# A gated-linear-attention and maxout kernel: w_out loaded whole ahead of w1, two sums of w2·w_out placed in the scores' banks, a first token group of two chunks, and another build-time order

## The chip, the cores and the metric

The kernel runs on one core of one Trainium2 chip. The metric is the device time of an execution in microseconds. The kernel before takes 147.35 us, the median of four runs (146.59, 146.69, 148.02 and 148.11). The profile is of one execution, which took 146.59 us.

The engines are called as in the profile: PE is TensorE (PEld its weight loads), DVE is VectorE, ACT is ScalarE, POOL is GpSimd, and SP is SyncE, whose queue (SPq) issues nearly all the transfers.

## The reference

Two steps follow each other. The first is a linear attention with a decaying state, for 4 batches of 8 heads, 768 positions and a head size of 48:

```python
for t in range(S):
    state = alpha[:, :, t, :, None] * state + np.einsum('bhd,bhe->bhde', k[:, :, t], v[:, :, t])
    y[:, :, t] = np.einsum('bhd,bhde->bhe', q[:, :, t], state)
```

Its output, with heads and head size joined, is x: 3072 tokens of 384 numbers. The second step is a feed-forward block with the larger of two projections, w1 and w2 of 384 x 1024 and w_out of 1024 x 384:

```python
g = np.maximum(x @ w1, x @ w2)
out = (g @ w_out).astype(np.float32)
```

Inputs and output are float32.

## The kernel before, in words

**The mathematics.** The larger of two numbers is written as max(a, b) = relu(a - b) + b. So the kernel computes h = x(w1 - w2), takes g = relu(h), and the output is g·w_out + x·M with M = w2·w_out. wd is w1 - w2 in float16, made on VectorE (`prep_wd`, L667, one instruction for each half of the 1024 columns). M is a matrix of 384 x 384 that is made once: w2 is cast (`prep_w2`), transposed by TensorE (`prep_t`, L677, the tile wtp) and copied to w2T (`prep_te`); w_out is cast (tile wo); then `prep_m` (L691, tile mp) sums eight matmuls for each of three blocks of rows, four in a first half (i = 0) and four in a second (i = 1), and the result is copied to m (operation `mev`).

**The attention in chunks.** Positions go in chunks of 128, 24 in all. In a chunk, the logarithms of alpha are summed by a matmul (cs), and exponentials of the sums with both signs (ep, en) scale q and k (qt and kt). These are transposed (tp), copied out (qk), and multiplied to scores (pa and pb, in two banks); the scores are masked on VectorE (pt), and y is summed from pt·v and from q times the state carried in (T, made by POOL from w and a decay). y is copied by ScalarE to xT. The first six chunks go in three double chunks, called d0, d1 and d2, by their own functions and with a d ahead of the tile's name: dloga, dcs, den, dep, dqt, dkt, dtp, dqk, dpa and dpb, dpt, dkv, dw, dT, dy.

**The feed-forward in groups.** Up to three finished chunks make a group. `fstep` (L702) makes h for 128 of the 1024 columns with three matmuls, so a group has eight such blocks of h; `relu` (L707 on VectorE, L709 on ScalarE) makes g. `tstep` makes the output of one chunk in a bank: three matmuls of x·M (L716) and eight of g·w_out (L719). The last chunk goes in two halves of columns (`tcols`). The output is evicted (L663, tile outs) and stored.

**Banks.** Three pools share the eight accumulation banks: psx with three (cs, tp, kv, wtp), psp with two (the scores pa and pb) and psm with three (y, h, op, and mp).

**Transfers.** All loads go through SP's queue in an order fixed by a chain of `after`: d0 in seven pieces, then w2 in two halves, w_out's first half, w1 in two halves, w_out's second half, d1, d2, and then the single chunks, four transfers each. The single chunks reuse the memory that held the weights in float32.

**Who sets the order.** No order is written by hand. Each piece of work is an `Op` with the engines that may run it, an assumed cost on each, what it depends on, the buffers that it takes, and a priority. `Sched.run` plays the program at build time: it keeps an assumed clock for each engine, picks the operation that can start first (a lower `prio` wins among equals), adds its cost, and emits its instructions. The order of instructions on each engine, and the choice between ScalarE and VectorE, thus follow from assumed costs; on the chip each engine runs its list strictly in that order. For a load, the assumed landing is made from the cost on a wire that all loads share (`LOAD`, `WLOAD / 2`, `DL`) and a latency (`lat`). For h and output work there is `refill`: it looks which chunks' xT is finished, and forms the next group of up to three. Chunk work has priorities near the chunk's number, h and output work 1000 and above, the sums of M 0.4.

Of the kernel before, what the change touches and what calls it, by code (L numbers as in the profile page):

```python
# [1 line left out]

# [7 lines left out]
FP32 = mybir.dt.float32  # L11
# [4 lines left out]
class Op:  # L16


    def __init__(self, sched, name, n, engs, fn, deps=(), lat=0.1, alloc=(), reads=(), prio=0.0, tiled=False, after=(), slack=0.0):
        self.name, self.n, self.engs, self.fn, self.lat = name, n, engs, fn, lat  # L20
        self.deps, self.alloc, self.prio, self.tiled = [d for d in deps if d is not None], list(alloc), prio, tiled
        self.after = [d for d in after if d is not None]
        self.done, self.slack = None, slack
        for b in list(alloc) + list(reads):
            b.users.append(self)
        for e in engs:
            sched.todo[e].append(self)
# [19 lines left out]
        return max(u.done for u in old.users)  # L47


class Sched:  # L50


# [4 lines left out]
    def __init__(self):  # L57
        self.todo = {e: [] for e in ("PE", "ACT", "DVE", "POOL", "SP")}
        self.free = {e: 0.0 for e in self.todo}
        self.wire = 0.0  # L60
        self.tiled = False
        self.refill = None

    def start(self, op):
        t = 0.0
# [42 lines left out]
    def run(self):  # L108
        while True:
            c = self.pick("PE")  # L110
            if c and self.refill:
                self.refill(c[1], c[1] > self.free["PE"] + 0.3)
            best = None
            for e in self.todo:
                c = self.pick(e)
                if c and (best is None or c[1] < best[0]):
                    best = (c[1], e, c[2])
            if best is None:
                if self.refill and self.refill(1e9, True):
                    continue  # L120
                break
            t, e, op = best
            cost = op.engs[e]
            if e == "PE" and t < 19.0:
                cost *= 1.9
            if e == "PE" and op.tiled != self.tiled:
                cost += 0.09
                self.tiled = op.tiled
            if e == "SP":
                t = max(t, self.wire - 4.0)  # L130
                self.wire = max(self.wire, t + 0.7) + cost
                op.done = self.wire + op.lat
                cost = 0.45
            else:
                op.done = t + cost + op.lat
            self.free[e] = t + cost
            for b in op.alloc:
                b.ring.taken.append(b)
            for x in op.engs:
                self.todo[x].remove(op)  # L140
            op.fn(e)
        assert not any(self.todo.values()), {e: [(o.name, o.n) for o in v][:5] for e, v in self.todo.items()}
# [3 lines left out]
def kernel(  # L146
# [23 lines left out]
    C = 128  # L170
# [5 lines left out]
    NT, DM = out.shape  # L176
    DFF = moe_w1.shape[1]
    NF = DFF // 128
    WMAX = 384
# [7 lines left out]
    psp = ctx.enter_context(tc.tile_pool(name="psp", bufs=2, space=bass.MemoryType.PSUM))  # L187
    psm = ctx.enter_context(tc.tile_pool(name="psm", bufs=3, space=bass.MemoryType.PSUM))
# [495 lines left out]
    mps = [None] * 3  # L684

    def prep_m(s, i):
        if i == 0:
            mps[s] = psm.tile([128, DM], FP32, tag="m", name="mp")
        mp = mps[s]
        for f in range(NFH * i, NFH * i + NFH):  # L690
            nc.tensor.matmul(mp, lhsT=w2T[:, f, s * 128 : (s + 1) * 128], rhs=wo16[:, f, :],  # L691
                             start=(f == 0), stop=(f == NF - 1))
# [62 lines left out]
    rx, rp, rm = Ring(3), Ring(2), Ring(3)  # L755
# [6 lines left out]
    def op(*a, **k):  # L762
        return Op(S, *a, **k)
# [3 lines left out]
    def dep(n, name):  # L767
        return G[n].get(name) if n in G else None

    LOAD, WLOAD = 1.06, 3.9  # L770
    bl = {}

    def loads_of(n):
# [9 lines left out]
    prev = None  # L783

    def dloads_of(m, margin):
# [3 lines left out]
        for i, h in parts:  # L789
            prev = op("dld", m, {"SP": DL / (1 if h is None else 2)}, lambda e, i=i, h=h: dload(m, i, h), lat=1.6 + margin,  # L790
                      alloc=[dbl[m][i]] if not h else (), reads=[dbl[m][i]] if h else (), after=[prev], prio=0.3 + m)
            for x in (0, 1):
                if h is None or h == x:
                    GD[m]["ld", i, x] = prev

    lw2, lw1, lwo = [None] * 2, [None] * 2, [None] * 2
    for x in "d0 w20 w21 wo0 w10 w11 wo1 d1 d2".split():
        if x[0] == "d":
            dloads_of(int(x[1]), 0.3 * int(x[1]))
        else:  # L800
            i = int(x[2])
            fn, to = {"w2": (load_w2, lw2), "wo": (load_wo, lwo), "w1": (load_w1, lw1)}[x[:2]]
            prev = to[i] = op(x, i, {"SP": WLOAD / 2}, lambda e, i=i, fn=fn: fn(i), lat=1.6, after=[prev], prio=0.5)


    w2c = [[op("w2c", (s, i), c, lambda e, s=s, i=i: prep_w2(e, s, i), deps=[lw2[i]], prio=-0.5)
# [13 lines left out]
    w2t = []  # L820
    for f in range(0, NF, 2):
        b = Buf(rx)
        t = op("w2t", f, {"PE": 0.4}, lambda e, f=f: prep_t(f), lat=0.17, deps=w2c[f // NFH], alloc=[b], prio=f - 10)
        w2t.append(op("w2te", f, {"DVE": 0.6, "ACT": 0.75}, lambda e, f=f: prep_te(e, f), deps=[t], reads=[b], prio=-0.4))
    mdone, mfirst = [], []
    for s in range(3):
        b = Buf(rm)
        prev = None
        for i in range(2):
            prev = op("m", s, {"PE": 0.66}, lambda e, s=s, i=i: prep_m(s, i), lat=0.17,  # L830
                      deps=w2t[2 * i : 2 * i + 2] + woc[2 * i : 2 * i + 2], after=[prev] if i else [],
                      alloc=[b] if i == 0 else (), reads=[b] if i else (), prio=0.4 + 0.01 * s)
            if i == 0:
                mfirst.append(prev)
        mdone.append(op("mev", s, {"ACT": 0.4, "DVE": 0.45}, lambda e, s=s: copy(e, m16[:, s, :], mps[s]),
                        deps=[prev], reads=[b]))
# [11 lines left out]
    for m in range(ND):  # L848
# [67 lines left out]
            alloc=[("y", 0), ("y", 1)], reads=[("pt", 0), ("pt", 1), ("qk", 0), ("qk", 1), "v", "T"], tiled=True)  # L916
        if m == 0:
            for o in mfirst:
                o.after.append(g["p4", 0])
        for u in range(2):  # L920
            G[2 * m + u]["a3"] = add("a3", u, {"ACT": 0.5}, lambda e, m=m, u=u: dx(m, u), [g["p4", 0]], reads=[("y", u)])

# [55 lines left out]
    def refill(now, idle):  # L978
        while pend and pend[0].done is not None:
            pend.pop(0)  # L980
        if len([o for o in pend if o.done is None]) > 2 or nxt[0] >= NCG:
            return
        if wdc[0][0].done is None or wdc[0][0].done > now + 0.3:
            return
        a = nxt[0]
        k = 0
        while k < WMAX // C and a + k < NCG and G[a + k]["a3"].done is not None and G[a + k]["a3"].done <= now + 0.3:
            k += 1
        if k == 0 or (k < WMAX // C and not idle):
            return  # L990
        nxt[0] += k
        W, a0 = k * C, a * C
        bg = Buf(rg16)
        rel = []
        xs = [G[a + i]["a3"] for i in range(k)]
        for f in range(NF):
            bh = Buf(rm)
            o = op("f", a, {"PE": 3 * max(W / 2400 + 0.0025, 0.07)}, lambda e, a0=a0, W=W, f=f: fstep(a0, W, f),
                   lat=0.17, deps=xs + wdc[f // NFH], after=pend[-1:], alloc=[bh] + ([bg] if f == 0 else []), prio=1000 + a)
            pend.append(o)  # L1000
            rel.append(op("relu", a, {"ACT": 0.08 + W / 1200, "DVE": 0.1 + W / 960},
                          lambda e, a0=a0, W=W, f=f: relu(e, a0, W, f), deps=[o], reads=[bh, bg], prio=n))
        for i in range(k):
            bo, bs = Buf(rm), Buf(ro)
            if a + i == NCG - 1:

                for c in range(2):
                    b = (bo, Buf(rm))[c]
                    o = op("t", a + i, {"PE": 0.95}, lambda e, a0=a0, i=i, c=c: tcols(a0, i, c), lat=0.17,
                           deps=mdone + woc + rel, after=pend[-1:], alloc=[b], reads=[bg], prio=1000 + a)  # L1010
                    pend.append(o)
                    ev = op("oev", a + i, {"ACT": 0.28}, lambda e, t=a0 + i * C, c=c: ocols(e, t, c), deps=[o],
                            alloc=[] if c else [bs], reads=[b, bs] if c else [b], prio=n)
                    op("st", a + i, {"ACT" if c else "SP": 0.3}, lambda e, t=a0 + i * C, c=c: scols(t, c), lat=1.2, deps=[ev],
                       reads=[bs], prio=-1)
                continue
            for half in range(2):
                o = op("t", a + i, {"PE": (0.98, 0.82)[half]}, lambda e, a0=a0, i=i, half=half: tstep(a0, i, half),
                       lat=0.17, deps=mdone + woc + (rel[:3] if half == 0 else rel), after=pend[-1:],
                       alloc=[bo] if half == 0 else (), reads=[bg] if half else [bg], prio=1000 + a)  # L1020
                pend.append(o)
            ev = op("oev", a + i, {"ACT": 0.4, "DVE": 0.45}, lambda e, t=a0 + i * C: oevict(e, t), deps=[o],
                    alloc=[bs], reads=[bo], prio=n)
            op("st", a + i, {"SP": 0.55}, lambda e, t=a0 + i * C: store(t), lat=1.2, deps=[ev], reads=[bs], prio=-1, slack=3.0 if a + i < NCG - 4 else 0.0)
        return True
# [34 lines left out]
```

## Time and profile before

| what | value |
|---|---|
| median of four runs | 147.35 us |
| the profiled execution: its own time / its span | 146.59 us / 144.8 us |
| busy PE / ACT / DVE / POOL | 130.7 / 99.0 / 86.5 / 83.5 us |
| PE idle in 0:10, 10:20, 20:30, 30:40 us of the span | 6.7, 2.5, 1.9, 0.0 us |
| h, op with w_out, op with M: matmuls and busy time | 216, 36.7 us; 184, 35.4 us; 69, 15.0 us |
| sums of M (mp): matmuls, first and last start | 24, 19.2 and 25.5 us |
| DMA: bytes, mean rate | 28.62 MB, 198 GB/s |

The span is the time from the first to the last instruction; the run's own time is longer by what lies around it. A busy time counts the time in which at least one instruction was under way; matmuls overlap, and a row's mean duration is that of one matmul from issue to modelled end, so the distance from start to start is the better measure of their cost. Forty slices of 3.62 us each show an engine's busy share in tenths. In a list of instructions, brackets give the idle time of the engine ahead of one, and what released it.

### The profile page before, as it was taken

What the parts mean: (1) busy time and instruction counts of PE and PEld (TensorE: products, weight loads), DVE (VectorE), ACT (ScalarE), POOL (GpSimd) and SP (SyncE); (2) the same over time, 40 slices, a digit from 0 to 9 for tenths busy, and PEclk for the clock granted to TensorE, in tenths of its full rate; (3) what the DMA queues carried; (4) which work ended last, traced back from release to release, by engine and by line L of the source; (5) the groups of instructions that cost most, each with busy time, mean ns of one, the idle gap of its engine ahead of it and who ended that gap; (6) DMA issues with size and microseconds to landing.
All of it is one profiled execution on the core that took longest, in us unless ns stands there. A gap on an engine that the chain in (4) does not pass through costs nothing.

```text
span 144.8 us, 4890 instructions
## 1 busy us (share of the span) xinstructions
PE 130.7 (90%) x1969; PEld 89.7 (62%) x1969; DVE 86.5 (60%) x163; ACT 99.0 (68%) x222; POOL 83.5 (58%) x184
## 2 busy tenths in 40 slices
PE   0375796899999999999999999999999999999991
PEld 0354653677777787666666667676666676556671
DVE  4648783688496679578539766699638854300000
ACT  4444844787686897879777977685768676825831
POOL 7997400587999788675559865657576955000000
PEclk9999999999999999999999999999999999999999
DMA  4999999999989797999999999999999722010213
GB/s 117 266 347 386 386 341 228 267 266 198 182 173 262 156 198 177 217 201 190 233 239 182 251 239 190 209 210 260 183 207 238 189 76 103 6 54 9 104 54 109
DMA packets 93686, 28.62 MB, mean 198 GB/s; under 512 B 87904, under 2 KB 92128, under 8 KB 93664
## 3 DMA queue, kind: packets, MB, share of 16 engines
q1 hardware_dynamic: 93520, 28.22, 81.9%
q8 instruction: 15, 0.25, 0.7%
q10 hardware_dynamic: 144, 0.10, 0.2%
q14 instruction: 7, 0.06, 0.1%
HBM read 23.59 MB, written 4.72 MB: 196 GB/s over the span
## 4 chain that ended last, share of the span: by engine, by line
PE 80%; DMA 9%; SPq 6%; ACT 2%; DVE 1%; issue 1%
PE h L702 22%; PE op L719 21%; DMA wof<-in_moe_w_out_dram 9%; PE op L716 8%; PE y L473 6%; PE pa L414 4%; PE tp L396 3%; SPq L231 3%; PE tp L398 3%; SPq L211 2%; PE cs L338 2%; PE kv L425 2%; PE dy L635 2%; PE mp L691 1%; PE dtp L541 1%; PE cs L342 1%
## 5 line engine op out<-in xcount | busy, mean ns | idle before, releaser
L702 PE MATMUL h<-xT,wd 128*128 128x384 f16 (+1 forms) x216 | 36.7, 308 | 0.0
L719 PE MATMUL op<-wo,g 128*128 128x384 f16 x184 | 35.4, 326 | 0.0
L709 ACT ACTIVATE g<-h 128x384 f16<-128x384 f32 (+1 forms) x53 | 24.1, 472 | 3.1 <-PE h L702 2.4
L702 PEld LDWEIGHTS <-wd 128*128 128x128 f16 x216 | 19.5, 97 | 9.3 <-issue 0.4
L719 PEld LDWEIGHTS <-g 128*128 128x128 f16 x184 | 17.2, 98 | 11.4
L663 ACT COPY outs<-op 128x384 f32<-128x384 f32 x20 | 9.6, 481 | 15.9 <-PE op L719 15.9
L433 DVE TENSOR_TENSOR pt<-pa,u 128x512 f16<-128x512 f32 x18 | 12.4, 690 | 7.7 <-PE pb L414 6.3
L375 POOL TENSOR_TENSOR T<-w,g 48x192 f16<-48x192 f32 x30 | 15.4, 514 | 1.1
L663 ACT COPY qk<-tp 128x1024 f16<-128x1024 f16 x14 | 14.2, 1016 | 2.3 <-PE tp L398 2.2
L716 PE MATMUL op<-m,xT 128*128 128x384 f16 x69 | 15.0, 326 | 0.0
L529 POOL TENSOR_TENSOR dkt<-dkf,den 128x384 f16<-128x384 f32 x6 | 6.3, 1050 | 10.9 <-ACT den L511 10.9
L433 DVE TENSOR_TENSOR pt<-pb,u 128x512 f16<-128x512 f32 x18 | 12.2, 680 | 0.1
L444 DVE TENSOR_TENSOR w<-kv,t 48x192 f32<-48x192 f32 x24 | 8.5, 352 | 5.9 <-PE kv L425 4.6
L707 DVE TENSOR_SCALAR g<-h 128x256 f16<-128x256 f32 (+1 forms) x19 | 9.0, 483 | 3.9 <-PE h L702 3.7
L348 ACT ACTIVATE en<-cs 128x384 f32<-128x384 f32 x18 | 8.9, 496 | 2.2 <-PE cs L342 2.2
L360 POOL TENSOR_TENSOR kt<-w2f,en 128x384 f16<-128x384 f32 x6 | 6.0, 1001 | 7.2 <-issue 2.6
L360 POOL TENSOR_TENSOR kt<-wof,en 128x384 f16<-128x384 f32 x6 | 6.5, 1087 | 6.1 <-ACT en L348 4.5
L477 ACT CAST xT<-y 128x384 f16<-128x384 f32 x18 | 8.7, 482 | 1.9 <-PE y L473 1.4
L360 POOL TENSOR_TENSOR kt<-w1f,en 128x384 f16<-128x384 f32 x6 | 6.0, 1002 | 5.5 <-issue 3.7
L473 PE MATMUL y<-pt,v 128*32 128x128 f16 x288 | 9.0, 220 | 0.0
L348 ACT ACTIVATE ep<-cs 128x384 f32<-128x384 f32 x18 | 8.9, 495 | 0.0
L716 PEld LDWEIGHTS <-xT 128*128 128x128 f16 x69 | 6.1, 98 | 3.1
(127 smaller groups left out, 281.5 us busy)
## 6 DMA issues: line engine op xcount, KB each, us to landing
out_dram<-outs SPq DMA_DIRECT2D x23, 192.0 KB, 3.3
w2f<-in_moe_w_dram SPq DMA_DIRECT2D x2, 768.0 KB, 7.2
wof<-in_moe_w_out_dram SPq DMA_DIRECT2D x2, 768.0 KB, 11.2
w1f<-in_moe_w_dram SPq DMA_DIRECT2D x2, 768.0 KB, 11.2
dvf<-in_v_dram SPq DMA_DIRECT2D x3, 384.0 KB, 5.9
wof<-in_alpha_dram SPq DMA_DIRECT2D x6, 192.0 KB, 3.8
wof<-in_k_dram SPq DMA_DIRECT2D x6, 192.0 KB, 4.1
wof<-in_q_dram SPq DMA_DIRECT2D x6, 192.0 KB, 4.5
```

The source lines that it names most:

```text
L348: nc.scalar.activation(out=t, in_=csv, func=ACTF.Exp, scale=scale)
L360: nc.gpsimd.tensor_mul(out=kts[n % NB][:, :, 0:D], in0=loads[n][1], in1=st[n]["en"])
L375: nc.gpsimd.tensor_mul(out=st[n]["T16"][ps, :, D * t : D * t + D], in0=st[n - 1]["w"][ps], in1=st[n]["g"][ps].unsqueeze(2).to_broadcast([D ...
L433: nc.vector.tensor_mul(out=s["pt"][:, t], in0=s["pp"][t], in1=ub)
L473: nc.tensor.matmul(y[o : o + 32, b // 4, :], lhsT=lhsT, rhs=rhs, start=start, stop=stop)
L477: nc.scalar.copy(out=xT[:, :, n * C : (n + 1) * C], in_=st[n]["y"])
L663: {"ACT": nc.scalar.copy, "DVE": nc.vector.tensor_copy, "POOL": nc.gpsimd.tensor_copy}[e](out=out, in_=in_)
L702: nc.tensor.matmul(h[:, 0:W], lhsT=wd16[:, s, f * 128 : (f + 1) * 128], rhs=xT[:, s, a : a + W], start=(s == 0), stop=(s == 2))
L707: nc.vector.tensor_relu(gts[a][:, f, 0:W], hs[a, f][:, 0:W])
L709: nc.scalar.activation(out=gts[a][:, f, 0:W], in_=hs[a, f][:, 0:W], func=ACTF.Relu)
L716: nc.tensor.matmul(op, lhsT=xT[:, s, t0 : t0 + C], rhs=m16[:, s, :], start=(s == 0), stop=False)
L719: nc.tensor.matmul(op, lhsT=gts[a][:, f, i * C : (i + 1) * C], rhs=wo16[:, f, :], start=False, stop=(f == NF - 1))
```

## The change

Five things change in the code.

- **Order of the loads.** The second half of w_out moves ahead of both halves of w1. The assumed cost of a weight load goes from 3.9 to 4.1 (for two halves) and its assumed latency from 1.6 to 2.0, 2.8 for w1's second half; the latency added for d0, d1 and d2 goes from 0, 0.3 and 0.6 to 0.2, 0.5 and 1.2.
- **Banks of mp.** The first two of the three mp tiles are taken from psp, the pool of the scores, and the third from psm as before.
- **Order of the sums of M.** Before, all first halves come after dy of d0 (`p4`) by the `after` list. Now they come after the second scores of d0 (`p3`, 1), and only the third tile's also after dy. The first halves of the first two tiles keep their priority; the third tile's first half and all second halves get 900. The third tile now depends on all of w2T and of wo.
- **First group.** `refill` may form the first group when two chunks are ready even where PE is not idle in the plan.
- **Jitter.** Each operation's assumed cost is multiplied by a factor drawn between 0.85 and 1.15 from a generator with a fixed seed. Only the planned times change by it.

```diff
@@ class Op
-        self.done, self.slack = None, slack
+        self.done, self.slack, self.scale = None, slack, 1.0 + JITTER * (sched.rng.random() - 0.5)
...
+SEED, JITTER = 107, 0.3
...
+        self.rng = random.Random(SEED)
@@ Sched.run
-            cost = op.engs[e]
+            cost = op.engs[e] * op.scale
@@ prep_m
-            mps[s] = psm.tile([128, DM], FP32, tag="m", name="mp")
+            mps[s] = (psp, psp, psm)[s].tile([128, DM], FP32, tag="ppm"[s], name="mp")
@@ loads
-    LOAD, WLOAD = 1.06, 3.9
+    LOAD, WLOAD = 1.06, 4.1
...
+    LANDS = {"w11": 2.8}
...
-    for x in "d0 w20 w21 wo0 w10 w11 wo1 d1 d2".split():
+    for x in "d0 w20 w21 wo0 wo1 w10 w11 d1 d2".split():
...
-            dloads_of(int(x[1]), 0.3 * int(x[1]))
+            dloads_of(int(x[1]), (0.2, 0.5, 1.2)[int(x[1])])
...
-            prev = to[i] = op(x, i, {"SP": WLOAD / 2}, lambda e, i=i, fn=fn: fn(i), lat=1.6, after=[prev], prio=0.5)
+            prev = to[i] = op(x, i, {"SP": WLOAD / 2}, lambda e, i=i, fn=fn: fn(i), lat=LANDS.get(x, 2.0), after=[prev], prio=0.5)
@@ sums of M
+    MPRIO = 900
     for s in range(3):
-        b = Buf(rm)
+        b = Buf((rp, rp, rm)[s])
...
-                      deps=w2t[2 * i : 2 * i + 2] + woc[2 * i : 2 * i + 2], after=[prev] if i else [],
-                      alloc=[b] if i == 0 else (), reads=[b] if i else (), prio=0.4 + 0.01 * s)
+                      deps=(w2t + woc if s == 2 else w2t[2 * i : 2 * i + 2] + woc[2 * i : 2 * i + 2]), after=[prev] if i else [],
+                      alloc=[b] if i == 0 else (), reads=[b] if i else (), prio=(0.4 if i == 0 and s < 2 else MPRIO) + 0.01 * s)
@@ double chunks
             for o in mfirst:
-                o.after.append(g["p4", 0])
+                o.after.append(g["p3", 1])
+            mfirst[2].after.append(g["p4", 0])
@@ refill
-        if k == 0 or (k < WMAX // C and not idle):
+        if k == 0 or (k < WMAX // C and not idle and (a or k < 2)):
```

More of the change, by code (lines that the diff above doesn't have):

```diff
@@ L2 @@
+import random
 from contextlib import ExitStack
```

## The prediction

> **What bounds the kernel now.** I read the page first: busy time per engine, then the forty slices.
>
> ```profile
> span 144.8 us, 4890 instructions
> PE 130.7 (90%) x1969; PEld 89.7 (62%) x1969; DVE 86.5 (60%) x163; ACT 99.0 (68%) x222; POOL 83.5 (58%) x184
> PE   0375796899999999999999999999999999999991
> DMA  4999999999989797999999999999999722010213
> ```
>
> TensorE (PE) is short of its span by 14.1 us, and the slices put nearly all of that into the first eight (3.62 us each). The busy times by stage say it in numbers (PE's busy time is the second figure after the stage):
>
> ```profile
> 10.00:20.00 10.00, 7.48 (x161) 5.68 (x158) 8.07 (x13) 5.84 (x11) 5.01 (x10) 1.00 1.05 383
> 20.00:30.00 10.00, 8.10 (x69) 5.51 (x68) 6.06 (x9) 5.93 (x15) 3.10 (x4) 1.00 1.07 260
> 30.00:40.00 10.00, 10.00 (x239) 7.20 (x240) 6.84 (x14) 7.16 (x20) 8.43 (x17) 1.00 1.06 210
> ```
>
> Idle PE: 6.7 us in 0:10, 2.5 in 10:20, 1.9 in 20:30, then none until the last matmul, and 3.0 us for the last eviction and store. So from 30 us on the end is a sum of PE work; only idle time ahead of it can go, unless the order inside the dense stretch hides small stalls. What the idle pieces are is in PE's list of instructions in order of time (start, length, then in brackets the idle time and its releaser):
>
> ```profile
> 12.94 0.80 PE L677 MATMUL wtp<-ident,w 128*128 128x128 f16 x6 [0.76 <-DVE dw L599]
> 15.22 0.31 PE L558 MATMUL dpa<-dqk 48*64 48x128 f16 x2 [1.48 <-ACT dqk L663]
> ...
> 19.25 3.26 PE L691 MATMUL mp<-wo,w2T 128*128 128x384 f16 x12
> 23.72 2.11 PE L691 MATMUL mp<-wo,w2T 128*128 128x384 f16 x12 [1.21 <-ACT wo L663]
> ...
> 26.53 1.14 PE L702 MATMUL h<-xT,wd 128*128 128x256 f16 x9
> 28.37 0.40 PE L541 MATMUL dtp<-ident,dqt 128*128 128x128 f16 x4 [0.69 <-DVE dqt L527]
> ```
>
> The 1.9 us of 20:30 are two waits: 1.21 for the second half of wo, 0.69 for dqt. The first is a transfer at bottom; the ScalarE list shows it, and a second case of the same kind:
>
> ```profile
> 13.63 0.62 ACT L663 CAST w<-w2f 128x512 f16<-128x512 f32 x1 [1.42 <-DMA w2f<-in_moe_w_dram]
> 14.16 1.01 ACT L663 COPY dqk<-dtp 128x1024 f16<-128x1024 f16 x1
> 22.84 0.83 ACT L663 CAST wo<-wof 128x768 f16<-128x768 f32 x1 [2.38 <-DMA wof<-in_moe_w_out_dram]
> ```
>
> dqk's input was whole at 12.18 (end of its transposes), but the copy stood behind a cast that waited for w2's second half.
>
> **The loads.** Issue plus time to landing of each: w2 first half 11.5, second 13.6, wo first 15.7, w1 17.8 and 19.8, wo second 22.8; then d1 (alpha 24.15, k 25.5, q 26.8, v 28.5). DMA is full from 2 us on, so a permutation of equal pieces (768 KB each) permutes these times. After: wo second 17.8, w1 first 19.8, w1 second 22.8; d1 has the same bytes ahead of it and stays.
>
> *Gain.* wo's second half is cast by 18.6 (0.83 us), so the 12 second-half mp matmuls need not wait until 23.7: the 1.21 us goes.
>
> *Cost.* wd, the difference w1 - w2 on VectorE (1.76 us each, started at 17.77 and 19.80), is ready at 21.6 and 24.6 instead of 19.5 and 21.6. What waits is h (L702), 8 blocks of three matmuls for the first two chunks: blocks 0 to 3 from 21.6, 4 to 7 from 24.6. The cover is mp: if PE starts it at 19.25 as before, its 24 matmuls end near 22.5 + 12 x 0.162 = 24.4; four blocks of h (12 x 0.113 = 1.4 us; from the 9 in 1.14 with the pipeline's tail of 0.16) bring 25.8, after 24.6. So the later wd costs nothing while mp covers it; without that cover (mp finished by 21) it would cost up to 3.6 us less 1.4 = 2.2. Behind wd's second half VectorE would hold back relus and evictions queued after it, at most its wait for the landing; ScalarE takes relus too. I put 0 to 0.5 us, and 0 as the value since the plan now lists that landing 0.8 us late.
>
> **mp in the scores' banks.** Before, three mp tiles take all three banks of the pool that h, y and op use, from 19.25 (the third when y is evicted at 20.4) until the evictions of m at 24.6 to 26.3. After, two lie in the scores' pool, free from the last mask of d0 (17.66) to the scores of d1 (30.68); one bank is left for mp's third tile, two for h from 20.4. That lets h start before mp is evicted. No instruction is added: 24 matmuls, 3 evictions. The two first halves may now go ahead of dy (17.82) while the others yield to chunk work. If they go first, dy and xT come later by up to 8 x 0.32 = 2.6 us; xT ends at 20.45 before, and h can't start before 21.6, so 1.1 us of that is free, 1.5 the worst. I take zero: masks free those banks at 17.0 and 17.66, when dy is ready too. The opposite price is d1's scores waiting for an eviction of m; the margin is 30.68 against about 25.6, 5 us: zero.
>
> **The 0.69 us for dqt.** The chain is dcs (25.67, behind mp), dep until 27.15, dqt until 28.2, dtp. dloga was ready at 25.09. With mp off PE by 24.4, dcs can start 0.58 earlier; the rest is a question of order, as h blocks lay ready at 28.2. With 24 h matmuls (2.7 us) and 22 op matmuls (22 x 0.1625 = 3.6 us) as filler from 21.6 on I take the whole 0.69 as removable.
>
> **The plan's clock.** The order is fixed at build time from assumed landings. By the code's numbers (0.7 start, 0.7 issue, wire cost, latency) the plan had w2's halves at 10.8 and 12.7, wo's at 14.7 and 20.5, d1's alpha at 22.3: 0.8 to 2.3 us before the trace. With 2.05 per half and a latency of 2.0 it has, ahead of the jitter, 11.3, 13.3, 15.4, 17.4, 19.5, 22.3 (with its own 2.8) and alpha at 23.1: within 0.5 for weights, 1.1 for d1. So the cast-before-dqk order is likelier to turn. If dqk goes at 12.2, it ends at 13.2; the scores' banks come free at 13.5 (masks on VectorE); dpa moves from 15.22 to 13.6. Bounds: 0 (order stays) to 1.6 us.
>
> Here a rule weighs. The PEclk row says full speed throughout, yet the first 12 mp take 3.26 us and the second 2.11. Starts lie 0.32 us apart at first and 0.16 from 21.6 on: seven at the slow spacing, four at the fast (7 x 0.32 + 4 x 0.16 = 2.9, plus the last's 0.33). The Trainium skill (TensorE: Matmul & The Clock Gate, "Part 1: The HAM clock gate") says that the array starts at half rate and is released after a busy window of about 3.4 us, windows running freely. It speaks against early filling: idle removed before the release buys half. By the plain row 1.6 us of gap would be worth 1.6; by the rule 0.8, which I take, at even odds: 0.4. The rule also gives a tail on both sides: release one window earlier or later is 3.4 x 0.5 = 1.7 us. The four runs shown (146.59, 146.69, 148.02, 148.11) differ by 1.4 between two pairs, which would fit, though no trace here shows it.
>
> **First group of two chunks.** Before, h is already 256 wide at 26.53, so two chunks went since PE was idle in the plan; now they may go without that. Width costs: per chunk 12 x 0.113 = 1.36 us against 24 x 0.163 / 3 = 1.30; there are three such groups in 72 matmuls. Likely none is added: 0 to 0.12 us for one more. **Jitter** scales each planned cost by 0.85 to 1.15, no instruction. In the dense stretch it may move stalls either way: bounded by the hidden stalls on the gain side (I count 110 us of start-to-start work in the 111.8 between 30 and 141.8, so 1.8) and by rival three on the other; taken as 0.
>
> **Downstream.** Work pulled out of 30:40 leaves a hole if dy of d1 (36.80; T and masks ready at 36.2) doesn't move too. Its v lands at 28.5; 0.6 us earlier dcs moves the masks; d2 lands 29.96 to 34.3 and was used from 31.4 to 36. I charge 0.3 us.
>
> Sum: 1.21 + 0.69 + 0.4 - 0.3 = 2.0 us. The profiled run took 146.59 (span 144.8 and 1.79 outside), so 144.6 on its scale. It is 0.76 under the median; the median of runs that split the same way is 147.35 - 2.0 = 145.35: I say 145.3.
>
> **Rivals.**
> 1. *The front fills* (chance 0.50), 143.8 to 146.0: the two stalls visible, the releasers known, and enough work to put there.
> 2. *The stall moves* (0.27), 146.0 to 147.9, about 146.9: PE gets ahead but data doesn't. DMA is full until 112 us, so d1, d2 and the first single chunks land when they did, and wd lands later. For it: dy of d1 was ready only 0.6 us before it ran. Then of 1.9 some 1.4 comes back as waits for wd (22 to 25), or for dpa and dy at 32 to 37. Against: from 50 us on h and op of several chunks stand ready as filler. That the order doesn't turn as thought belongs here: the time stays.
> 3. *The new order stalls later* (0.23), slower: PE takes instructions in order, so a block planned ahead of a producer that is late blocks all. The present plan has no visible stall in 112 us; planned costs lie near measured ones (kt 1.0 against 1.00 to 1.09, h 0.487 against 0.488), and a 15% error on kt, qk copies and masks (about 1.0 + 1.0 + 1.4 us in one chain) is 0.5 us, over the plan's margin of 0.25. The front's stalls averaged 0.85 us (0.78, 0.19, 0.76, 1.48, 1.21, 0.69); five such among 18 chunks are 4.2. Time 147.35 - 2.0 + 4.2 = 149.5; it decides from 2.0 us of stall between 30 and 141. Against: abundant filler.
>
> Range: 143.8 to 149.0, which leaves out the far part of rival 3 and little below; the likeliest case alone is 143.8 to 146.0. One per cent, 1.5 us, is about what a measurement of this kernel can tell from no change: faster 0.50, same 0.27, slower 0.23.
>
> **What would show it.** Right: the wait mp on wo gone; h starting near 21.6 to 24 rather than 26.5; PE idle in 20:30 under 0.5 us; PE's end 2 us earlier with the same busy time. dpa before 14 would show the plan's clock at work. Wrong: PE waits on DVE wd at 22 to 25; a wait of dy or dpa at 30 to 37; new PE waits after 40. A release of the clock at another time than 21.6, read from the spacing of mp, would move the time without the change's doing.

## The result

The changed kernel takes 146.37 us (median of 43 runs, 144.85 to 149.01), the kernel before 147.2 us (64 runs). The ratio is 0.9935 with a 95% interval of 0.9918 to 0.9952: 0.65% less time, 0.7 to 1.2 us. That is clear of no change, and below the one per cent under which the forecast spoke of "same". The forecast of 145.3 us was a gain of 2.0 us; a little under half of it came. 146.4 lies where the prediction put rival 2, "the stall moves". (Runs that lie well above their kernel's fastest are left out of every ratio; where the profiled execution of an experiment is such a run, the text says how far it lies above its median.)

The page of the changed kernel, first lines and the shares of the chain that ended last:

```profile
span 144.6 us, 4886 instructions
PE 130.3 (90%) x1969; PEld 88.5 (61%) x1969; DVE 90.0 (62%) x170; ACT 98.2 (68%) x216; POOL 82.3 (57%) x183
PE   0378995599999999999999999999999999999991
PE h L708 21%; PE op L725 21%; PE op L722 8%; SPq L217 7%; DMA dqf<-in_q_dram 6%; PE y L479 5%; PE pa L420 4%; SPq L237 4%; PE tp L402 3%; PE tp L404 3%; PE cs L344 2%; PE kv L431 2%; PE dy L641 2%; PE dtp L547 1%; PE cs L348 1%
```

PE's slices show what happened: the fourth to sixth show 8, 9 and 9 tenths (5, 7 and 9 before), then come two of 5, where the kernel before had 6 and 8. The chain no longer runs through the load of wo (9% before) but through the load of q for d1. The stages (PE's busy time second):

```profile
10.00:20.00 10.00, 9.26 (x181) 6.37 (x174) 5.62 (x12) 7.05 (x11) 4.29 (x7) 1.00 1.05 382
20.00:30.00 10.00, 6.97 (x65) 4.98 (x64) 6.83 (x8) 5.88 (x16) 3.20 (x5) 1.00 1.05 250
30.00:40.00 10.00, 9.68 (x243) 6.95 (x241) 7.70 (x13) 7.54 (x19) 8.14 (x16) 1.00 1.13 223
```

PE idles 0.7 us in 10:20 (2.5 before), but 3.0 in 20:30 (1.9 before) and 0.3 in 30:40 (none before). PE's own list in order of time says on what:

```profile
13.46 0.32 PE L564 MATMUL dpa<-dqk 48*64 48x128 f16 x2
...
16.25 1.50 PE L697 MATMUL mp<-wo,w2T 128*128 128x384 f16 x4
...
18.62 3.42 PE L697 MATMUL mp<-wo,w2T 128*128 128x384 f16 x20
22.38 1.16 PE L708 MATMUL h<-xT,wd 128*128 128x256 f16 x9 [0.33 <-DVE wd L673]
24.74 0.24 PE L502 MATMUL dcs<-dloga,c 128*128 128x192 f16 x1 [1.21 <-ACT dloga L492]
...
25.60 1.49 PE L708 MATMUL h<-xT,wd 128*128 128x256 f16 x12
28.58 0.40 PE L547 MATMUL dtp<-ident,dqt 128*128 128x128 f16 x4 [1.49 <-DVE dqt L533]
```

The wait for wo is gone, dpa runs at 13.46 instead of 15.22, all mp is done at 22.0 instead of 25.8, and h starts at 22.4 instead of 26.5. Then PE stands three times: for wd, for dloga, for dqt. Behind these stand transfers, in the lists of VectorE and ScalarE:

```profile
20.56 1.76 DVE L673 TENSOR_TENSOR wd<-w1f,w2f 128x1536 f16<-128x1536 f32 x1 [2.06 <-DMA w1f<-in_moe_w_dram]
22.70 1.76 DVE L673 TENSOR_TENSOR wd<-w1f,w2f 128x1536 f16<-128x1536 f32 x1 [0.38 <-DMA w1f<-in_moe_w_dram]
27.45 1.08 DVE L533 TENSOR_TENSOR dqt<-dqf,dep 128x384 f16<-128x384 f32 x1 [0.90 <-DMA dqf<-in_q_dram]
```

```profile
24.17 0.94 ACT L492 ACTIVATE dloga<-daf 128x384 f16<-128x384 f32 x2 [1.60 <-DMA daf<-in_alpha_dram]
25.01 0.64 ACT L715 ACTIVATE g<-h 128x256 f16<-128x256 f32 x2
```

The last line matters too. Three blocks of h were finished by 23.5 and filled three banks. Their relus stood behind wd's second half on VectorE (22.70 to 24.46) and behind dloga on ScalarE, which waited 1.6 us for alpha; the first relu ran at 24.38. So PE had no bank for a fourth block before that, whatever stood next in its list.

**A ledger of PE's work.** Busy time can't show which of two kernels is further along. So I counted the matmuls started by a given time and weighed each kind with its spacing at full speed: 0.1625 us for 384 columns, 0.1135 for 256, 0.0555 for 128 and for transposes, the small tiled ones (scores, y, kv) likewise from their spacing. This makes 121.4 us for the whole kernel. The table gives the work done by the kernel before, in its first profile, and the lead over it in the first profile of each other kernel (minus: behind). The 40 matmuls added in `warm` are not counted. It holds for single profiled executions.

| work by time (us) | 24 | 30 | 38 | 45 | 60 | 130 |
|---|---|---|---|---|---|---|
| before, work done | 7.36 | 12.55 | 20.16 | 26.79 | 41.40 | 109.80 |
| changed | +2.65 | +1.11 | +0.60 | +0.48 | +0.30 | +0.36 |
| loads_only | +1.62 | +0.90 | +0.93 | +0.17 | -0.19 | +0.20 |
| banks_only | +0.70 | +1.11 | +1.04 | -0.08 | -1.26 | -0.94 |
| jitter_0 | +2.31 | +1.43 | +1.21 | -0.74 | -1.97 | -1.68 |
| seed_1 | +1.97 | +1.60 | +1.60 | +0.49 | -0.84 | -1.10 |
| seed_2 | +2.31 | +2.04 | +0.87 | 0.00 | -0.58 | -0.51 |
| d1_planned_late | +2.99 | +3.22 | +0.60 | -0.11 | -0.43 | +0.10 |
| warm | +0.33 | +0.35 | +0.21 | -0.33 | -1.10 | -0.94 |
| no_w11 | +2.98 | +3.03 | +2.62 | +2.14 | +2.20 | +2.31 |
| before_again | +0.65 | +0.56 | +0.52 | +0.49 | +0.33 | +0.39 |
| changed, after_again | +1.62 | +0.35 | +0.32 | -0.98 | -1.14 | -0.94 |

The changed kernel is 2.65 us ahead at 24 us; 1.5 of it is gone at 30, another 0.6 at 45, and from then on nothing much changes to the end. Part of the 2.65 need not be the change's doing, as the moment of the release moves between profiles of one kernel too: in this profile the fast spacing began at about 17.5 us, in the first of before at 21.6, and four microseconds of work at twice the pace are worth up to 2 us (an estimate from these spacings). So the question was who takes the lead back between 24 and 60 us.

### The profile page after: what moved, and what is told of

It reads as the page before. It is cut to its first block, busy times and chain, and to the rows that moved or that the text cites. A ratio compares the mean times of both kernels' runs of the same rounds, so it can differ in the third digit from the quotient of the medians.

```text
span 144.6 us, 4886 instructions
## 1 busy us (share of the span) xinstructions
PE 130.3 (90%) x1969; PEld 88.5 (61%) x1969; DVE 90.0 (62%) x170; ACT 98.2 (68%) x216; POOL 82.3 (57%) x183
## 4 chain that ended last, share of the span: by engine, by line
PE 76%; SPq 12%; DMA 6%; DVE 2%; ACT 1%; issue 1%; DVEq 0%; ACTq 0%
PE h L708 21%; PE op L725 21%; PE op L722 8%; SPq L217 7%; DMA dqf<-in_q_dram 6%; PE y L479 5%; PE pa L420 4%; SPq L237 4%; PE tp L402 3%; PE tp L404 3%; PE cs L344 2%; PE kv L431 2%; PE dy L641 2%; PE dtp L547 1%; PE cs L348 1%
## 5 line engine op out<-in xcount | busy, mean ns | idle before, releaser
L713 DVE TENSOR_SCALAR g<-h 128x384 f16<-128x384 f32 (+1 forms) x28 | 14.1, 515 | 13.8 <-PE h L708 13.7
L715 ACT ACTIVATE g<-h 128x384 f16<-128x384 f32 (+1 forms) x44 | 19.5, 456 | 3.3 <-PE h L708 2.9
L669 ACT COPY qk<-tp 128x1024 f16<-128x1024 f16 x17 | 17.2, 1013 | 4.6 <-PE tp L404 4.3
L669 ACT COPY outs<-op 128x384 f32<-128x384 f32 x16 | 7.7, 478 | 14.6 <-PE op L725 14.5
L366 POOL TENSOR_TENSOR kt<-wof,en 128x384 f16<-128x384 f32 x6 | 6.0, 999 | 8.0 <-ACT en L354 7.1
L502 PE MATMUL dcs<-dloga,c 128*128 128x192 f16 x6 | 1.6, 270 | 7.2 <-ACT dloga L492 7.2
```

What stands on the lines that cost most here:

```text
L366: nc.gpsimd.tensor_mul(out=kts[n % NB][:, :, 0:D], in0=loads[n][1], in1=st[n]["en"])
L669: {"ACT": nc.scalar.copy, "DVE": nc.vector.tensor_copy, "POOL": nc.gpsimd.tensor_copy}[e](out=out, in_=in_)
L713: nc.vector.tensor_relu(gts[a][:, f, 0:W], hs[a, f][:, 0:W])
L715: nc.scalar.activation(out=gts[a][:, f, 0:W], in_=hs[a, f][:, 0:W], func=ACTF.Relu)
```

## The experiments

Theory S: the supply takes it. The bytes that go through the queue ahead of d1 and the following chunks fix when PE's work exists, so PE only reaches the waits sooner. Rivals: the drawn order (O), a plan with wrong landings (P), PE's clock (G), and losses in the dense stretch (D). All ratios are to the kernel before on the same chip. The kernel before, measured a second time against itself (below), strays by 0.37%; a difference between two ratios of that size says little.

### 768 KB less, the order of instructions kept

```diff
     def load_w1(i):
-        load_w(moe_w1, w1f, slice(i * FH, (i + 1) * FH))
+        if i == 0:
+            load_w(moe_w1, w1f, slice(i * FH, (i + 1) * FH))
...
-        nc.vector.tensor_sub(out=wd16[:, :, c], in0=w1f[:, :, c], in1=w2f[:, :, c])
+        nc.vector.tensor_sub(out=wd16[:, :, c], in0=w1f[:, :, 0:FH], in1=w2f[:, :, c])
```

> The changed kernel with its order of instructions kept on every engine, but the load of w1's second half left out (768 KB) and wd's second half made from w1's first half, so the output is not the reference's. Theory S (supply): after the change PE is ahead of its data at 22 to 28.5 us, and d1's landing sets the pace. Then d1's alpha lands near 22.2 instead of 24.2 and its q near 25.4 instead of 27.4; PE's idle time in 22:29 falls from 3.0 us to 1.2 or less, and the time falls by 1 to 2 us against the changed kernel (144.4 to 145.4 against its median of 146.4). Rival D (the dense stretch takes it back): the lead that PE gains in front is lost before 60 us as it was in the changed kernel (1.1 us at 30, 0.5 at 45), and the time falls by 0.5 us or less.

144.78 us, ratio 0.9812 (0.9762 to 0.9863): 1.24% below the changed kernel's 0.9935, 1.8 us. d1's alpha landed at 22.2 and its q at 25.7. PE's list:

```profile
22.73 1.16 PE L709 MATMUL h<-xT,wd 128*128 128x256 f16 x9
24.73 1.49 PE L709 MATMUL h<-xT,wd 128*128 128x256 f16 x12
26.47 0.40 PE L548 MATMUL dtp<-ident,dqt 128*128 128x128 f16 x4 [0.25 <-DVE dqt L534]
```

With the same instructions in the same order the waits for wd and dloga are gone and that for dqt is 0.25, and the stage 20:30 has 9.60 us of PE work instead of 6.97. The lead of 3.0 us at 30 is still 2.2 at 60 and 2.3 at 130. Rival D's total falls, since the time fell by 1.8 us where it allowed 0.5. But of its lead this kernel lost 0.8 us between 30 and 60, and the changed kernel lost 0.8 there too. What the bytes explain is the 1.5 us that the changed kernel lost before 30 and this one did not; the 0.8 stays without a cause. The edit makes wd's second half ready earlier as well as bringing d1 forward, so it shows what the bytes are worth, not which of the two waits mattered.

### The same in the kernel before

The edit is the same, in the kernel before.

> The kernel before with its order kept, the load of w1's second half left out (768 KB) and wd's second half made from w1's first half, so the output is not the reference's. w_out's second half and d1 then land about 2 us earlier. Theory S: the kernel before is held by the same bytes, and gains what the changed kernel gained by it, 1.2 to 2.2 us (145.0 to 146.1), its wait for wo gone or below 0.3 us. Rival (only the changed kernel had come to its supply, the one before was held by its order): the kernel before gains less than 1.0 us.

Ratio 0.9848 (0.9796 to 0.9899), 1.5% or 2.2 us less than the kernel before; median 146.23. Its wait for wo is 0.34 us, just over what was expected. So the kernel before hangs on the same bytes; the rival falls. (Its profiled execution lies 1.3 us above its median and is read for this wait alone.)

### 768 KB more, the order kept

```diff
         load_w(moe_w1, w1f, slice(i * FH, (i + 1) * FH))
+        if i == 1:
+            load_w(moe_w1, spare, slice(0, FH))
```

> The changed kernel with its order kept on every engine, and one load more on SP's queue: w1's first half a second time (768 KB), into a spare tile that nothing reads, between w1's second half and d1. The opposite of leaving a load out. Theory S (bytes ahead of d1 and of what follows set the time): d1 and all later chunks land about 2 us later, PE's idle time in 22:31 grows by 1.5 to 2 us, and the time rises by 1.2 to 2.2 us against the changed kernel (147.6 to 148.6). Rival: what lost the lead was the order, and the filler (h, op) absorbs later data; the time rises by less than 0.6 us.

148.48 us, ratio 1.0049 (1.0022 to 1.0075): 1.1% above the changed kernel, 1.7 us; the filler does not hide it. The wait for dloga, in a profiled execution 2.1 us above the median, and the stages behind it (the last three figures of a stage: granted clock, DMA share, GB/s):

```profile
28.23 0.32 PE L505 MATMUL dcs<-dloga,c 128*128 128x192 f16 x1 [2.98 <-ACT dloga L495]
```

```profile
28.00:30.00 2.00, 1.77 (x18) 1.62 (x18) 0.00 (x0) 1.99 (x8) 0.23 (x1) 0.50 0.92 231
30.00:32.00 2.00, 2.00 (x11) 1.40 (x10) 1.44 (x2) 1.09 (x6) 1.99 (x3) 0.50 0.98 248
```

A weight half takes 2.0 to 2.1 us to land behind the one ahead of it (in each kernel one of them takes longer, mostly about 3). Taking one out moved the times by -1.8 and -2.2 us: near one for one. The +1.7 of the load put in is of the same size, but it is not landing time alone: after the long wait PE's granted clock fell to half, and it was below full in 19 of this kernel's 23 runs, against 2 of 44 of the changed kernel. The four runs at full clock took 146.84 to 148.68 us; they are too few to part the two.

### Other draws of the order

```diff
-SEED, JITTER = 107, 0.3
+SEED, JITTER = 107, 0.0    (jitter_0);  1, 0.3 (seed_1);  2, 0.3 (seed_2)
```

> The changed kernel with the jitter at zero: loads, banks, sums of M and the first group are as changed, the plan runs on its own costs. Theory S: the gain comes from the loads and banks in front; without jitter the time is within 0.5 us of the changed kernel (145.9 to 146.9). Rival O (the drawn order): the draw of this seed is worth more than the rest; without it the kernel is 1 us or more slower than the changed one (147.4 or more), with new PE waits after 30 us.

> The changed kernel with the generator's seed at 1 in place of 107, nothing else. Theory S: within 0.5 us of the changed kernel, since the front's waits are set by landings. Rival O: another draw is 1 to 3 us slower, with single PE waits of 0.3 to 1.5 us after 30 us.

> The changed kernel with the seed at 2. As for seed 1: within 0.5 us by theory S, 1 to 3 us slower by rival O. The two draws and the run without jitter together give how far an order by itself moves the time.

jitter_0: 148.68 us, ratio 1.0068 (1.0038 to 1.0099). seed_1: 147.57 us, 1.0012 (0.9983 to 1.0041). seed_2: 147.82 us, 1.0029 (1.0002 to 1.0057). All three are 0.8 to 1.3% above the changed kernel, 1.1 to 2.0 us, and none is faster than the kernel before. Here I was wrong, and rival O right: loads, banks, sums and group are the same in all four, and without this seed's draw they give nothing. In the ledger the three lead by as much as the changed kernel or more at 30, and fall further behind by 60. PE's waits between 34 and 60 us, in the run without jitter:

```profile
41.72 0.33 PE L708 MATMUL h<-xT,wd 128*128 128x128 f16 x3 [1.51 <-ACT g L715]
47.85 0.33 PE L708 MATMUL h<-xT,wd 128*128 128x128 f16 x3 [0.28 <-DVE g L713]
48.74 0.50 PE L708 MATMUL h<-xT,wd 128*128 128x128 f16 x6 [0.24 <-ACT g L715]
54.96 0.32 PE L344 MATMUL cs<-loga,cmat 128*128 128x384 f16 x1 [0.41 <-ACT loga L339]
```

and with seed 1:

```profile
41.43 0.32 PE L344 MATMUL cs<-loga,cmat 128*128 128x384 f16 x1 [1.08 <-ACT loga L339]
...
55.25 0.32 PE L344 MATMUL cs<-loga,cmat 128*128 128x384 f16 x1 [0.76 <-ACT loga L339]
```

In this stretch PE's visible waits sum to 2.4 us (jitter_0), 2.0 (seed_1), 1.4 (seed_2) and 0.3 in the changed kernel (h for xT, at 38.05). loga is the first step of a single chunk. In seed_1 it was itself waiting, on ScalarE:

```profile
40.85 0.52 ACT L339 ACTIVATE loga<-wof 128x384 f16<-128x384 f32 x1 [1.36 <-DMA wof<-in_alpha_dram]
...
54.67 0.52 ACT L339 ACTIVATE loga<-w1f 128x384 f16<-128x384 f32 x1 [0.88 <-DMA w1f<-in_alpha_dram]
```

So in seed_1 the supply sets the pace in these places too; that an order is good when it has other work there is my reading. jitter_0 and seed_2 also form groups of a single chunk (48 matmuls of 128 columns, ten groups instead of nine). In jitter_0 PE waits 2.0 us for relus of these short blocks; in seed_2 its waits are others (0.85 for dT, 0.35 for xT, 0.17 for outs).

The rule on the first group needs no run: with that line undone, the plan comes out with the same instructions in the same order on all five engines. With this draw it does nothing.

### Single parts of the change

Both in the kernel before; loads_only:

```diff
-    LOAD, WLOAD = 1.06, 3.9
+    LOAD, WLOAD = 1.06, 4.1
...
-    for x in "d0 w20 w21 wo0 w10 w11 wo1 d1 d2".split():
+    for x in "d0 w20 w21 wo0 wo1 w10 w11 d1 d2".split():
...
-            dloads_of(int(x[1]), 0.3 * int(x[1]))
+            dloads_of(int(x[1]), (0.2, 0.5, 1.2)[int(x[1])])
...
-... lat=1.6, after=[prev], prio=0.5)
+... lat=LANDS.get(x, 2.0), after=[prev], prio=0.5)
```

> The kernel before with the new order of the loads and their new assumed landings alone (w_out whole ahead of w1; costs and latencies as changed); banks, sums of M, first group and costs as before. Theory S: the PE wait for the second half of wo (1.21 us) is gone, and dqk goes ahead of the cast of w2's second half; new waits for wd, dloga or dqt take part of it. Time 0.3 to 1.2 us below the kernel before. Rival O: no gain (within 0.3 us) or slower, since the order drawn from the new plan outweighs it.

146.87 us, ratio 1.0001 (0.9968 to 1.0035): no gain. The wait for wo is gone as expected, and this came in its place:

```profile
24.85 0.24 PE L496 MATMUL dcs<-dloga,c 128*128 128x192 f16 x1 [1.38 <-ACT dloga L486]
27.57 0.49 PE L702 MATMUL h<-xT,wd 128*128 128x256 f16 x3 [0.72 <-ACT g L709]
```

1.21 and 0.69 us went, 1.38 and 0.72 came, and this execution took 146.56 us against 146.59 of the first profile of before: in one profile, at full clock, this is the exchange. The ratio of 1.0001 is less clean: in 12 of the 14 runs the granted clock was below full (the table under "PE's clock"), and the two others took 146.40 and 146.56. How much of the missing gain is the clock is not shown. banks_only:

```diff
-            mps[s] = psm.tile([128, DM], FP32, tag="m", name="mp")
+            mps[s] = (psp, psp, psm)[s].tile([128, DM], FP32, tag="ppm"[s], name="mp")
...
-        b = Buf(rm)
+        b = Buf((rp, rp, rm)[s])
...
-                o.after.append(g["p4", 0])
+                o.after.append(g["p3", 1])
+            mfirst[2].after.append(g["p4", 0])
```

with the sums' dependences and priorities as changed.

> The kernel before with the change of banks and of the order of the sums of M alone: two mp tiles in the scores' pool, second halves and the third tile late, w_out's second half still loaded last. Theory S: the second halves of mp still can't start before wo's second half lands at 22.8, but PE can run h from 19.5 on, since two banks are free; the wait of 1.21 us goes by filling, and the time is 0.3 to 1.2 us below the kernel before. Rival: nothing fills, since relus queue behind the casts of wo; within 0.3 us of before.

147.87 us, ratio 1.0075 (1.0045 to 1.0104): slower by 1.1 us. Two banks for h did not fill the wait:

```profile
23.46 2.11 PE L691 MATMUL mp<-wo,w2T 128*128 128x384 f16 x12 [1.30 <-ACT wo L663]
```

wo lands last here, so the second halves of mp wait at the head of PE's queue as before. This order too has groups of one chunk, with waits for relus at 40.5 and 48.9 (0.56 and 0.31 us). Neither theory had it slower; a new plan is a new draw, with or without jitter.

### d1 planned when it lands

```diff
-            dloads_of(int(x[1]), (0.2, 0.5, 1.2)[int(x[1])])
+            dloads_of(int(x[1]), (0.2, 1.6, 2.3)[int(x[1])])
```

> The changed kernel with the assumed landing of d1 and d2 raised by 1.1 us, to what its trace shows for d1's alpha (24.2 against 23.1 planned). Theory P (the plan): the 1.21 us wait for dloga and the 1.49 us for dqt are PE instructions planned 1.1 us too early while h and op blocks are there; planned late, PE's idle time in 22:29 falls from 3.0 us to 1.5 or less, and the time falls by 0.5 to 1.5 us against the changed kernel. Theory S alone: there is too little work without d1's data (relus stand behind wd and dloga, three banks full), PE's idle time stays at 2 us or more, and the time stays within 0.5 us.

The front did what theory P says: the stage 20:30 has 9.40 us of PE work, the idle time is 0.6, and the lead at 30 us is 3.2. The time did not: 146.95 us, ratio 0.9991 (0.9961 to 1.0022), 0.8 us above the changed kernel by the ratios. I missed both ways: there was enough work without d1 (against S), and it paid nothing (against P). In this order ScalarE runs three relus from 23.13 on, ahead of its work on d1's alpha, and so frees the banks. The next double chunk takes it:

```profile
35.37 0.40 PE L547 MATMUL dtp<-ident,dqt 128*128 128x128 f16 x4 [1.47 <-DVE dqt L533]
```

and after it PE's granted clock is at half (the last three figures of a stage: clock, DMA share, GB/s):

```profile
34.00:36.00 2.00, 0.63 (x9) 0.58 (x10) 2.00 (x3) 1.02 (x4) 1.86 (x3) 0.96 0.89 161
36.00:38.00 2.00, 2.00 (x94) 1.56 (x91) 1.40 (x3) 1.86 (x4) 2.00 (x4) 0.50 0.77 148
38.00:40.00 2.00, 2.00 (x51) 1.65 (x35) 1.66 (x3) 1.76 (x5) 1.87 (x4) 0.69 1.13 267
```

PE had nothing else from 33.9. This dqt is of d2: its q had landed at 32.7, its dep was ready at 33.6 and VectorE free at 33.8, so even the load alone, with the 1.0 us of a dqt, would have let dtp start at 33.7 at best; the rest is the chain behind alpha (29.8), and this dqt took 1.52 us where d1's took about 1.1. By 40 us the lead was 0.0. The clock has its part in that: the three stages fall short of full by 0.08, 1.00 and 0.62 us, 1.7 together, and the wait is 1.5; the lead lost from 30 to 40 is 3.2. I read the wait so: the filler spent at 22 to 28 us is missing at 34. Since the clock fell in 12 of this kernel's 14 runs, what the later plan would give with the clock held is open.

### PE's clock

```diff
     def dcs(m, h):
+        if m == 0:
+            burst((20, 14)[h])      # 128-column matmuls on a spare tile
...
     def dp(m, h):
+        if m == 0 and h == 0:
+            burst(6)
```

> The changed kernel with 40 added matmuls on a spare tile in PE's idle time ahead of 10 us (20 and 14 ahead of the two first sums of logarithms, 6 ahead of the first scores), the planned order kept. They show what the release of PE's clock is worth: PE should be at its fast spacing by 10 us instead of 18.3. Theory S: PE only gets dry sooner; idle time in 20:29 grows by as much as the work ahead of it shrinks, h still starts at 22.4, and the time stays within 0.4 us of the changed kernel. Rival G (the clock): the front's work at half rate is worth 1 us or more, and the time falls by 0.8 to 1.7 us; the spread of the runs gets smaller too.

147.0 us, ratio 0.9966 (0.9930 to 1.0003): not below the changed kernel, so the gain that rival G expected did not come; 0.45 us above it by the ratios, at the edge of what S allowed, and within what a repeat strays. The release did come early (dcs at 7.0 us with its matmuls 0.08 us apart instead of 0.16), but the clock fell back, and mp met the slow array again:

```profile
10.00:20.00 10.00, 5.93 (x82) 4.07 (x81) 4.57 (x10) 5.22 (x9) 4.27 (x7) 0.63 1.05 383
```

So what a clock held open through the front would be worth stays open.

There is a second way for the clock to matter: it can fall again after it was released. The mean granted clock of each run tells. Most runs show 0.997 to 1.000; the others show 0.989 or less. At 0.988, 145 us lack 1.7 us of clock, just what the three stages of d1_planned_late lack.

| kernel | runs | below 0.99 | median of the others (us) |
|---|---|---|---|
| before, beside the experiments | 131 | 9 | 147.5 |
| changed | 44 | 2 | 146.4 |
| no_w11; before_no_w11 | 6; 6 | 0; 0 | 144.8; 146.2 |
| banks_only | 11 | 0 | 147.9 |
| seed_2 | 22 | 2 | 147.8 |
| seed_1 | 22 | 7 | 147.5 |
| jitter_0 | 19 | 5 | 148.3 |
| loads_only | 14 | 12 | 146.5 |
| d1_planned_late | 14 | 12 | 146.6 |
| extra_load | 23 | 19 | 148.3 |
| warm | 14 | 10 | 147.6 |

So the fall goes with the kernel. It does not explain the other draws, which by these medians lie 1.1 to 1.9 us above the changed kernel at full clock too. What it costs is not settled: in before, the changed kernel, jitter_0 and seed_2 the runs with it are 1.0 to 2.2 us longer at the median, in loads_only, d1_planned_late, extra_load and seed_1 0.2 to 0.5, and in warm shorter, each time with few runs on one side.

### Both kernels once more

> The kernel before, unchanged, for a second profile. Where PE's clock is released can lie elsewhere than at 21.6 us, read from the spacing of the mp matmuls (0.32 against 0.16 us). Theory S: the time is within 0.3 us of the kernel before, and PE's work done by 60 us differs by less than 0.8 us between the two profiles though the release differs. Rival G (the clock): a release 3.4 us apart shows as 1 us or more of PE work at 60 us and in the time of the profiled run.

> The changed kernel, unchanged, for a second profile, and a second measurement of its gain on a chip shared with the runs above. Theory S: ratio to the kernel before 0.991 to 0.997; PE's lead over the kernel before is 1 to 2.5 us at 24 to 30 us and under 0.7 us at 60 us, as in the first profile, wherever the clock is released. Rival: lead and loss lie elsewhere in the second profile, and the first one's account is of that run alone.

before_again: ratio 0.9963 (0.9925 to 1.0000) to its own kernel's runs, 14 runs: 0.5 us, more than the 0.3 that I allowed, and a measure of how far such a comparison strays. after_again: 0.9895 (0.9851 to 0.9938), 6 runs. The gain is there again; the figure of 43 runs stands, though it is less than twice what the repeat of one kernel strayed.

In the second profile of the kernel before the clock was released earlier, and the wait for wo grew:

```profile
19.18 2.26 PE L691 MATMUL mp<-wo,w2T 128*128 128x384 f16 x12
23.16 2.11 PE L691 MATMUL mp<-wo,w2T 128*128 128x384 f16 x12 [1.72 <-ACT wo L663]
```

The first twelve mp took 1.0 us less than in the first profile, the wait 0.5 us more, wo landed 0.56 earlier, and that run took 146.29 against 146.59: rival G's microsecond doesn't show. The second profile of the changed kernel missed the expected ledger: the lead is 1.62 at 24, 0.35 at 30 and -1.14 at 60. Its loads were late from the start (w2's first half on VectorE, first and second profile):

```profile
11.22 0.43 DVE L669 CAST w<-w2f 128x512 f16<-128x512 f32 x1 [0.20 <-DMA w2f<-in_moe_w_dram]
```

```profile
12.93 0.43 DVE L669 CAST w<-w2f 128x512 f16<-128x512 f32 x1 [1.80 <-DMA w2f<-in_moe_w_dram]
```

1.7 us at w2, still 1.7 at d1's alpha (24.17 and 25.86), and the run took 147.66 us against 146.36. PE's waits of the front are the same three (0.70 for wd, 0.83 for dloga, 0.54 for dqt). But 1.3 us more went between 38 and 45 us, where the first profile lost 0.1; 0.67 of it is a wait for loga at 42.96. To that extent the rival came true: the account of the front holds in both profiles, that of the stretch behind it only in the first.

## Why the prediction was right in sign and too large

The range and the sign held; the likeliest case did not. That the sign held is in part luck: the draw was taken at nothing, and with any of three other draws the same change is not faster than the kernel before.

- **The wait for wo (1.21 us)** went, as said, in the changed kernel and in loads_only.
- **The plan's clock.** The turn of dqk and the cast came, and dpa moved to 13.46 (13.6 was said). Taken at even odds, it happened in full.
- **The later wd at no cost** failed. The landings did not simply change places: w1's first half came at 20.54 instead of 19.8, so wd's first half was ready at 22.3 instead of 21.6. The cover was mp, and it was to last to 24.4. It was over at 22.0: some of mp went ahead of dy, and in that run the array ran at its fast spacing from about 17.5 us, not 21.6 (20 mp in 3.42 us; before, 12 took 3.26). The case without cover was priced in the prediction, at up to 2.2, and not taken. The price of relus queued behind wd (0 to 0.5, taken as 0) was more: VectorE was busy with wd while ScalarE waited 1.6 us for dloga's alpha.
- **The 0.69 us for dqt, "the whole removable"** failed. It grew to 1.49 and got a companion of 1.21 for dloga. dcs came 0.93 us earlier, but dqt hangs on q, which landed at 27.35 (before, 26.8; the prediction had d1's landings stay). I had named the plan's error of 1.1 us for d1 and not drawn what follows: PE instructions placed in good time by the plan are 1.1 us early on the chip.
- **Downstream, 0.3 us** was too small. From 30 to 60 us the changed kernel lost 0.8 of 1.1 and no_w11 0.8 of 3.0, so earlier bytes do not cure it; 0.3 is PE's wait for xT at 38.05, the rest is open. The kernel with a full front, d1_planned_late, lost 3.6 of 3.2, 1.7 of it at a lower clock.
- **Jitter taken as 0** was wrong in another way. It isn't neutral: three other draws cost 1.1 to 2.0 us more. The bound of 1.8 us on the gain side had room for it (by the ledger it should have been 2.9: 121.4 less 12.55 is 108.9 us of work, not 110); nothing in the profile of before could tell which draw this is.

So rival 2 was the right mechanism. Of its places 22 to 25 us was right; 32 to 37 was not, as the changed kernel waits at 28.6 and 38.05 instead. Its reading of the sum: the front's gain is for the most part given back (in the profile of loads_only all of it), and the 0.65% that remains goes with this draw of the order. Why this draw is better than three others is shown only as far as its fewer waits between 34 and 60 us; its first profile is 0.2 us faster than the first one of before, less than the medians differ, so the rest stays open. No version here beats the changed kernel with the whole computation done.

## What to carry to other kernels

Where the transfers are full from the start, ask of each removed wait which load comes next, and when it lands; here a permutation of loads for the most part renamed the wait, while a load less was worth about its full landing time. Compare two kernels by work done at a given time, not by idle time: that shows where a lead is lost. And when a planner orders the work, measure a few plans that differ by nothing but a draw before crediting a gain of one per cent to a part of the change, and look at the granted clock of every run, not of the profiled one alone.

## What the runs showed of the hardware

- The runs of one kernel don't fall into the two pairs that four of them suggested: 64 runs of before spread evenly from 146.06 to about 148.2. Two profiles of the changed kernel differ by 1.7 us in when the first weight half lands, and by 1.3 us in the run's time; in 8:10 of the span the transfers moved 355 GB/s in the first and 316 in the second.
- PE's fast spacing began at about 17.5, 19.5 and 21.6 us in three profiles of two kernels, with the clock row at full speed throughout. The row shows a closed clock only once it has been open (warm 0.63 in 10:20, d1_planned_late 0.50 in 36:38 after 1.5 us of waiting). That the release moves from run to run is what the Trainium skill says (TensorE: Matmul & The Clock Gate, "Part 1: The HAM clock gate"); it gives 0.5 us to either side for a run of equal matmuls, and here two profiles of the kernel before, 21.6 and 19.5, lie 2 us apart. That so short a wait in a dense stretch can close it I had not expected.
- In some of these kernels the clock falls again in almost every run (d1_planned_late and loads_only, 12 of 14 each), in others hardly ever (the changed kernel, 2 of 44).
